# Where the operands of the spatial products lie in SBUF, and the order of work at the stage's two borders

## The chip, the cores and the metric

The kernel runs on one NeuronCore of a Trainium2 chip. The metric is the device time of one execution in microseconds (us). Of the kernel before there are three timed runs, with a median of 613.38 us (613.30 to 613.72), and one profiled execution.

## The reference

Two branches read the same normalised input and are added to it. All tensors are float32; there are S = 2048 rows, D = 512 columns, H = 32 heads of 16, and Fh = 688 gate columns.

```python
xn = layernorm(x)
# branch A: linear attention with a learned feature map
q, k, v = heads(xn @ wqkv)
phi(t) = concat(softmax(t @ w_phi), softmax(-(t @ w_phi)))     # per head
o = phi(q) @ (phi(k).T @ v) / (phi(q) @ sum_s(phi(k)) + 1e-6)
a = o @ wo
# branch B: spatial gate
z = gelu(xn @ w_in)                                            # 2 x 688 columns
z2 = layernorm(z[:, 688:])
g = w_sp @ z2 + b_sp[:, None]                                  # 2048 x 2048 by 2048 x 688
b = (z[:, :688] * g) @ w_out
out = x + a + b
```

The spatial product `w_sp @ z2` is the largest one.

## The kernel before, in words

**Arithmetic.** Every large product is made of three matmuls (`mm3`, lines 55 to 59): each operand is split into a rounded part h and a rest l, and hh, hl and lh are summed in PSUM. ScalarE rounds (`round_h`, line 49 of the profile), VectorE subtracts for the rest (`rest_l`, line 53). In a matmul the left operand is the 128x128 weight that is loaded into the array, and the right one is streamed through it.

**Stages.** The first stage makes the projections q, k and v of all 16 row tiles, the softmaxes, the sums over k, and the first gate half z1, which is kept in DRAM. The second (lines 737 to 768) makes z2, row tile by row tile: four PSUM pools in turn take the projection `zps` (`zproj`), ScalarE applies gelu, VectorE takes the statistics, GpSimd the reciprocal root, ScalarE normalises (`normed`). The third is the spatial stage (lines 887 to 926), with the products `g`. The last (lines 1075 to 1103) makes the two output projections into `pout`, and the attention's `po`.

**The spatial stage.** It uses Strassen's scheme in Winograd's form: 2x2 blocks of the left matrix with 2x2 blocks of the right one need seven products instead of eight. There are 32 chunks n. Eight groups i of 256 output rows have four quarters q each; chunk n is (i, q), and the last group takes its quarters in the order 1, 2, 3, 0 (`SEQ`, line 590). One chunk is seven products with two contraction steps k of three matmuls: 42 matmuls of 344 columns. `FORM` (line 776) gives the order: P1 = A11 B11, P2 = A12 B21, P6 = S2 T2, P5 = S1 T1, P7 = S3 T3, P3 = S4 B22, P4 = A22 T4. Seven of the eight PSUM banks hold the sums of a group, and the next group begins in the eighth.

**Left operands.** `load_a(n)` brings the chunk's two raw blocks over SP's DMA queue, and `prep_a(n)` makes from them A11, A12, A22 and the sums S1 to S4, in h and l. The raw blocks have two buffers. The finished tiles have two rooms, `hl[0]` (in the pool `ws`, at the right end of SBUF) for even n and `hl[1]` (at the end of the left pools) for odd n, so chunk n + 2 overwrites chunk n. The sums are made in a tile of their own, `S`.

**Right operands.** `b_split` makes B11, B21, B22 and T1 to T4 out of two finished row tiles of z2, for each of eight pairs of row tiles (2q + k). A B tile (`b_tile`, lines 694 to 703) is 5632 bytes of each partition: h and l, each with two operands of 344 columns of which every one has 352 words, that is 1408 bytes. Ten of the tiles are in the pools `xz2a` and `xz2`, five each; sixteen in the room of `xT` as it comes free; two in `xz3`.

**Order.** The program is traced in the order of the code; a scheduler then orders the instructions of each engine by its own cost model, gives out the slots of the pools, and sets the semaphores. A tile waits until all that used its room before is done. `tc.issue_after(ins)` puts the instructions of a block behind `ins` on the same engine.

**Drain.** When a group is done, ScalarE and VectorE combine its seven sums into four blocks (`drain`), `gate` multiplies them with gelu of z1, and the result goes through DRAM in transposed form for the last stage. During the last four chunks the last stage's first weights and operands are loaded (`stage_w`, `first_gate`), and the room of the left pools behind `xz` becomes the pools `cw` and `cwk`.

Of the kernel before, what the change touches and what calls it, by code (L numbers as in the profile page):

```python
# [10 lines left out]
F32 = mybir.dt.float32  # L11
# [7 lines left out]
P = 128  # L19
# [22 lines left out]
def mixer(ctx: ExitStack, tc: tile.TileContext, x, x_t, wv, wqkT, phi_bd, wo, w_in, wst, b_r, w_out, out):  # L42
# [50 lines left out]
    cst.tile([P, 8], F32, name="pad")  # L93
# [44 lines left out]
    def zproj(ps, s, w, order=(0, 1), wide=False):  # L138
# [405 lines left out]
    mid.enter_context(right("pad", 1)).tile([P, P + 8], F32, name="pad")  # L544
# [5 lines left out]
    w2_pool.tile([P, QP // 2], F32, name="gap")  # L550
# [45 lines left out]

    def load_a(n):
        i, q = SEQ[n]
        f = []
        for k in range(2):  # L600
            t = ws.tile([P, QC, P], F32, tag=f"f{k}", bufs=2, name="wf")
            sp.dma_start(t, wst[2 * i + k, :, q * QC:(q + 1) * QC, :])
            f.append(t.rearrange("p (k two) t -> p two k t", two=2))
        return f

    def prep_a(n, f):

# [10 lines left out]
        sums = (sm[0].tile([P, 4, 2, P], F32, name="S") if sm else  # L618
                zw.tile([P, 4, FC], F32, tag=("T", "z2")[n], bufs=n + 1, name="S").rearrange("p a b -> p (a b)")[:, :8 * P].rearrange("p (a k b) -> p a k b", a=4, k=2))
        parts(("A11", "A12"), a)  # L620
        dve.tensor_tensor(sums[:, 0], b[:, 0], b[:, 1], op=ALU.add)
        dve.tensor_tensor(sums[:, 1], sums[:, 0], a[:, 0], op=ALU.subtract)  # L622
# [7 lines left out]
    hl, raw, A, sm = [ws, None], {}, {}, []  # L630
    NE = 2
    with ExitStack() as p1:
# [40 lines left out]
        A[0] = prep_a(0, raw.pop(0))  # L673
        sp.dma_start(kvT_d, kvT)
# [30 lines left out]
    B, b11 = [], None  # L705

    def b_split(z, n):
        nonlocal b11
        tt = zw.tile([P, 4, FC], F32, tag="T", name="T")
        dve.tensor_tensor(tt[:, 0:2], z[:, 1:3], z[:, 0:2], op=ALU.subtract)  # L710
        if n % 2 == 0:
            b11 = b_tile()
        b_parts(b11[:, 0, n % 2], b11[:, 1, n % 2], z[:, 0])
        dve.tensor_tensor(tt[:, 2], z[:, 2], tt[:, 0], op=ALU.subtract)
# [23 lines left out]
    for s in range(NT):  # L738
        p = zproj((kv_ps_p, zc, zbp, za)[s % 4], s, w2, (0, 1) if s % 2 == 0 else (1, 0), s == 0)
# [397 lines left out]
```

## Time and profile before

| what | value |
| --- | --- |
| median of three runs | 613.38 us |
| the profiled execution, its own time | 613.14 us |
| its span, from first to last instruction | 611.4 us |
| TensorE busy | 605.8 us (99%) |
| TensorE weight loads busy | 551.9 us (90%) |
| VectorE busy | 519.9 us (85%) |
| ScalarE busy | 259.7 us (42%) |
| GpSimd busy | 132.4 us (22%) |
| granted TensorE clock | 1.00 throughout |

The busy time of an engine is the union of its instructions' times. A matmul of 344 columns is listed with some 319 ns and one of 512 with some 390 ns, but matmuls overlap in a pipeline: the next one starts long before the one before it has ended. What a matmul costs is the distance from its start to the next one's, which is called the beat here. It is read from the timeline, whose rows give start, duration, engine, line, operation, written and read tiles, shapes, a count, and the idle time of the engine before it with the instruction that ended it.

### The profile page before, as it was taken

What the parts mean: (1) busy time and instruction counts of PE and PEld (TensorE: products, weight loads), DVE (VectorE), ACT (ScalarE), POOL (GpSimd) and SP (SyncE); (2) the same over time, 40 slices, a digit from 0 to 9 for tenths busy, and PEclk for the clock granted to TensorE, in tenths of its full rate; (3) what the DMA queues carried; (4) which work ended last, traced back from release to release, by engine and by line L of the source; (5) the groups of instructions that cost most, each with busy time, mean ns of one, the idle gap of its engine ahead of it and who ended that gap; (6) DMA issues with size and microseconds to landing.
All of it is one profiled execution on the core that took longest, in us unless ns stands there. A gap on an engine that the chain in (4) does not pass through costs nothing.

```text
span 611.4 us, 11387 instructions
## 1 busy us (share of the span) xinstructions
PE 605.8 (99%) x4286; PEld 551.9 (90%) x4286; DVE 519.9 (85%) x930; ACT 259.7 (42%) x414; POOL 132.4 (22%) x231
## 2 busy tenths in 40 slices
PE   8999999999999999999999999999999999999997
PEld 7888888888888999999999999999999978777776
DVE  5999999999988578899888896877879999999932
ACT  4653324423433547887534434342345443332220
POOL 4122232323111014552000001000200041143430
PEclk9999999999999999999999999999999999999999
DMA  8557776566537848001445636455566799699882
GB/s 316 191 130 178 215 178 188 146 166 167 142 102 218 259 179 306 5 1 35 143 122 154 172 100 184 135 164 152 167 161 202 247 314 269 186 288 278 210 217 69
DMA packets 57950, 107.85 MB, mean 176 GB/s; under 512 B 12392, under 2 KB 24552, under 8 KB 57672
## 3 DMA queue, kind: packets, MB, share of 16 engines
q1 hardware_dynamic: 43656, 65.22, 34.6%
q0 software_dynamic: 11936, 36.28, 23.9%
q10 hardware_dynamic: 2304, 5.64, 2.4%
q8 instruction: 33, 0.54, 0.4%
q14 instruction: 21, 0.17, 0.1%
HBM read 66.85 MB, written 35.54 MB: 167 GB/s over the span
## 4 chain that ended last, share of the span: by engine, by line
PE 96%; DVE 1%; DMA 1%; issue 0%; POOL 0%; ACT 0%; POOLq 0%
PE g L57 12%; PE g L58 11%; PE g L59 11%; PE proj L57 7%; PE proj L58 7%; PE proj L59 7%; PE zps L57 6%; PE zps L59 6%; PE zps L58 6%; PE pout L57 6%; PE pout L59 5%; PE pout L58 5%; PE po L1003 1%; PE pout L1017 1%; DMA zacc<-e 1%; PE kvps L373 1%
## 5 line engine op out<-in xcount | busy, mean ns | idle before, releaser
L57 PE MATMUL g<-B,A 128*128 128x344 f32 x448 | 142.4, 319 | 0.0
L58 PE MATMUL g<-B,A 128*128 128x344 f32 x448 | 142.4, 319 | 0.0
L59 PE MATMUL g<-B,A 128*128 128x344 f32 x448 | 138.9, 318 | 0.0
L57 PEld LDWEIGHTS g<-B,A 128*128 128x128 f32 x448 | 84.1, 188 | 0.3 <-ACT A L49 0.3
L58 PEld LDWEIGHTS g<-B,A 128*128 128x128 f32 x448 | 84.0, 188 | 0.0
L59 PEld LDWEIGHTS g<-B,A 128*128 128x128 f32 x448 | 83.6, 188 | 0.0
L49 ACT ACTIVATE A<-S 128x512 fp32r<-128x512 f32 x64 | 39.3, 628 | 73.7 <-DVE S L622 54.1
L57 PE MATMUL proj<-wqk_h,xT 128*128 128x512 f32 x128 | 50.1, 391 | 0.0
L59 PE MATMUL proj<-wqk_h,xT 128*128 128x512 f32 x128 | 49.8, 389 | 0.0
L58 PE MATMUL proj<-wqk_l,xT 128*128 128x512 f32 x128 | 49.8, 389 | 0.0
L125 ACT ACTIVATE e<-e,r_x 128x1024 f32<-128x1024 f32 x26 | 29.8, 1149 | 42.3 <-DVE e L124 41.3
L53 DVE TENSOR_TENSOR A<-S,A 128x512 fp32r<-128x512 f32 x64 | 42.8, 683 | 2.9 <-ACT A L49 2.8
L49 ACT ACTIVATE A<-wf 128x512 fp32r<-128x512 f32 (+1 forms) x64 | 32.8, 515 | 25.4 <-DMA wf<-in_wst 20.8
L57 PE MATMUL zps<-w1h,xT 128*128 128x344 f32 (+2 forms) x128 | 40.8, 320 | 0.0
L59 PE MATMUL zps<-w1h,xT 128*128 128x344 f32 (+2 forms) x128 | 40.7, 318 | 0.0
L57 PE MATMUL zps<-w2h,xT 128*128 128x344 f32 (+2 forms) x128 | 40.7, 318 | 0.0
L58 PE MATMUL zps<-w1l,xT 128*128 128x344 f32 (+2 forms) x128 | 40.6, 318 | 0.0
L58 PE MATMUL zps<-w2l,xT 128*128 128x344 f32 (+2 forms) x128 | 40.6, 317 | 0.0
L59 PE MATMUL zps<-w2h,xT 128*128 128x344 f32 (+2 forms) x128 | 40.3, 317 | 0.0
L53 DVE TENSOR_TENSOR A<-wf,A 128x512 fp32r<-128x512 f32 (+1 forms) x64 | 35.0, 549 | 4.8 <-ACT A L49 4.8
L128 DVE TENSOR_REDUCE sm<-e 128x64 f32<-128x1024 f32 x26 | 31.1, 1199 | 2.5 <-ACT e L125 2.5
L787 POOL DMA_DIRECT2D z1t<-z_d x16 | 9.1, 595 | 108.6 <-DMA wf<-in_wst 98.1
(219 smaller groups left out, 1434.9 us busy)
## 6 DMA issues: line engine op xcount, KB each, us to landing
wf<-in_wst SPq DMA_DIRECT2D x64, 256.0 KB, 3.4
e_d<-e POOLq DMA_DIRECT2D x16, 544.0 KB, 5.0
et<-e_d SPq DMA_DIRECT2D x16, 544.0 KB, 7.6
z_d<-z1f ACTq DMA_DIRECT2D x16, 344.0 KB, 3.4
z1t<-z_d POOLq DMA_DIRECT2D x16, 344.0 KB, 4.6
zacc<-e POOLq DMA_DIRECT2D x10, 512.0 KB, 4.8
u<-u_d SPq DMA_DIRECT2D x15, 320.0 KB, 6.2
xt<-in_x SPq DMA_DIRECT2D x16, 256.0 KB, 3.7
```

What stands on the lines that cost most here:

```text
L49: return act.activation(h, src, AF.Copy).ins
L53: return (eng or dve).tensor_tensor(l, src, h.bitcast(F32), op=ALU.subtract).ins
L57: pe.matmul(dst, ah, bh, start=start, stop=False)
L58: pe.matmul(dst, ah, bl, start=False, stop=False)
L59: return pe.matmul(dst, al, bh, start=False, stop=stop).ins
L125: softmax_pair.last = less, act.activation(e, e, AF.Exp, scale=scale).ins
L128: dve.tensor_reduce(sm, heads(e), axis=AX.X, op=ALU.add)
L373: i = pe.matmul(kv_acc[k:k + QP, m // 4], vs[:, m * QP:(m + 1) * QP], e[:, m * HP:(m + 1) * HP], start=first and m < 4 and len(ready) == n ...
L787: pool.dma_start(t[:, k, :FH], z1_d[2 * i + k])
L1003: lasts[3] = pe.matmul(po[r][c * QP:(c + 1) * QP, k], kvT[rows, m // 2, cols], fs[m // 4][rows, m // 2 % 2], start=True, stop=True).ins
L1017: lasts[2] = pe.matmul(p, rt, w, start=False, stop=i == NT - 1 and k == 1).ins
```

## The change

It has four parts.

1. **Addresses.** Some paddings get other sizes: the constants' pad of 8 words goes, the pad at the right end of SBUF shrinks from 136 to 16 words, the gap at the end of `w2` grows from 16 to 48 words, and a pad of 32 words stands ahead of `hl[1]`. Within a chunk the left operands are laid out in another order, S4 S3, A22, A11 A12, S2 S1, with 32 words more in the tile of A11 and A12, where A11 starts 32 words later when the quarter is even. `spread` changes one step of an access pattern. Of the right operands, B21 now comes first in its tile and B22 second, and a tile of B11 is shared by the quarters q and q + 1 of the same k, and not by the two k of one quarter.
2. **Sums in place.** S1 to S4 are written over the raw blocks, once A11, A12 and A22 have been rounded. The tile `S` goes. There are three raw tiles (f and x in `ws`, y in the room of `zw`) and loads are asked for four chunks ahead, not three.
3. **The border between second and third stage.** The left operands of chunks 1 and 2 are prepared ahead of the last three normalisations and the last two splits, and chunk 0's products are traced ahead of these. The third raw load is traced earlier, behind chunk 0's preparation. The first subtraction of a late split is put behind chunk 1's sums.
4. **Drain and last stage.** The block c22 is made of P7 and c12, no longer of P5 and c21. The PSUM pool of the last stage's output is opened first, with its first tile, and the pool of transposes behind it. The tiles of the pool `cw` come in another order.

```diff
-    cst.tile([P, 8], F32, name="pad")
...
-    mid.enter_context(right("pad", 1)).tile([P, P + 8], F32, name="pad")
+    mid.enter_context(right("pad", 1)).tile([P, HP // 4], F32, name="pad")
...
-    w2_pool.tile([P, QP // 2], F32, name="gap")
+    w2_pool.tile([P, QP + HP // 4], F32, name="gap")
...
+    def spread(ap, axis, more):
+        dims = [list(d) for d in ap.ap]
+        dims[axis][0] += more
+        return bass.AP(ap.tensor, ap.offset, dims)
+
     def load_a(n):
         i, q = SEQ[n]
-        f = []
+        tag = "fx"[n] if n < 2 else "fxy"[(n - 2) % 3]
+        t = (fy[0] if tag == "y" else ws).tile([P, 2, QC, P], F32, tag="wf" + tag, name="wf")
         for k in range(2):
-            t = ws.tile([P, QC, P], F32, tag=f"f{k}", bufs=2, name="wf")
-            sp.dma_start(t, wst[2 * i + k, :, q * QC:(q + 1) * QC, :])
-            f.append(t.rearrange("p (k two) t -> p two k t", two=2))
-        return f
+            sp.dma_start(t[:, k], wst[2 * i + k, :, q * QC:(q + 1) * QC, :])
+        return [t[:, k].rearrange("p (k two) t -> p two k t", two=2) for k in range(2)]
...
+        for names, more in ((("S4", "S3"), 0), (("A22",), 0), (("A11", "A12"), QP), (("S2", "S1"), 0)):
+            tiles[names] = pl.tile([P, D * len(names) + more], F32R, tag="".join(names), name="A")
+
         def parts(names, src):
-            t = pl.tile([P, 2, len(names), 2, P], F32R, tag="".join(names), name="A")
-            prep_a.last = b_parts(t[:, 0], t[:, 1], src)
+            late = QP * (1 - SEQ[n][1] % 2) if "A11" in names else 0
+            more = QP if "A11" in names else 0
+            t = tiles[names][:, late:late + D * len(names)].rearrange("p (m l k t) -> p l m k t", l=2, k=2, t=P)
+            h, l = (spread(t[:, v], 1, more - late) for v in range(2))
+            prep_a.last = b_parts(h, l, src)
             for k, m in enumerate(names):
-                ops[m] = t[:, 0, k], t[:, 1, k]
+                ops[m] = h[:, k], l[:, k]
...
         parts(("A11", "A12"), a)
-        dve.tensor_tensor(sums[:, 0], b[:, 0], b[:, 1], op=ALU.add)
-        dve.tensor_tensor(sums[:, 1], sums[:, 0], a[:, 0], op=ALU.subtract)
-        parts(("S1", "S2"), sums[:, 0:2])
-        dve.tensor_tensor(sums[:, 2], a[:, 0], b[:, 0], op=ALU.subtract)
-        dve.tensor_tensor(sums[:, 3], a[:, 1], sums[:, 1], op=ALU.subtract)
-        parts(("S3", "S4"), sums[:, 2:4])
         parts(("A22",), b[:, 1:2])
+        a11, a12, a21, a22 = a[:, 0], a[:, 1], b[:, 0], b[:, 1]
+        dve.tensor_tensor(a22, a21, a22, op=ALU.add)
+        dve.tensor_tensor(a21, a11, a21, op=ALU.subtract)
+        dve.tensor_tensor(a11, a22, a11, op=ALU.subtract)
+        prep_a.summed = dve.tensor_tensor(a12, a12, a11, op=ALU.subtract).ins
+        parts(("S2", "S1"), pair(a11, a22))
+        parts(("S4", "S3"), pair(a12, a21))
...
         A[0] = prep_a(0, raw.pop(0))
+        prep_a.first = None
+        raw[2] = load_a(2)
         sp.dma_start(kvT_d, kvT)
...
-        if n % 2 == 0:
-            b11 = b_tile()
-        b_parts(b11[:, 0, n % 2], b11[:, 1, n % 2], z[:, 0])
+        k, q = n % 2, n // 2 % 2
+        if not q:
+            b11[k] = b_tile()
+        b = b11[k][:, 0, q], b11[k][:, 1, q]
+        b_parts(*b, z[:, 0])
...
-        if s == NT - 1:
-            for k in range(2):
-                normed(*late.pop(0), ins)
     ctx_w2.__exit__(None, None, None)
     x3.append(mid.enter_context(ctx_x3))
     hl[1] = mid.enter_context(left("hl1", 1))
+    hl[1].tile([P, QP], F32, name="pad")
     A[1] = prep_a(1, raw.pop(1))
-    raw[2] = load_a(2)
-    normed(*late.pop(), ins)
-    ctx_zw.__exit__(None, None, None)
+    prep_a.first = prep_a.summed
+    raw[3] = load_a(3)
...
+    products(0, g)
+    A[2] = prep_a(2, raw.pop(2))
+    while late:
+        normed(*late.pop(0), ins)
+    ctx_zw.__exit__(None, None, None)
+    gt = mid.enter_context(right("gt", 1))
+    fy.append(mid.enter_context(right("fy", 1)))
...
         dve.tensor_tensor(c12, g["P5"], c21, op=ALU.add)
+        add(c22, g["P7"], b2, c12)
         dve.tensor_tensor(c21, g["P7"], c21, op=ALU.add)
-        add(c22, g["P5"], b2, c21)
...
-    er_pair("er")
-    wo_h = cw.tile([P, ND, D], F32R, name="woh")
+    f_pair()
+    cw.tile([P, KF * P], F32, tag="u", bufs=4, name="u")
     cw.tile([2 * REM, P], F32R, tag="rt", bufs=6, name="rt")
+    wo_l = cw.tile([P, ND, D], F32R, name="wol")
     cw.tile([P, D], F32, tag="wof", bufs=4, name="wof")
     kvT = cw.tile([P, 2 * NG, HP], F32, name="kvT")
-    cw.tile([P, KF * P], F32, tag="u", bufs=4, name="u")
-    wo_l = cw.tile([P, ND, D], F32R, name="wol")
+    wo_h = cw.tile([P, ND, D], F32R, name="woh")
...
+    pso = ctx.enter_context(psum("pso", 1))
+    pout = [pso.tile([P, D], F32, tag="out", bufs=2, name="pout")]
     pst = ctx.enter_context(psum("pst", 4))
-    pso = ctx.enter_context(psum("pso", 1))
```

More of the change, by code (lines that the diff above doesn't have):

```diff
@@ L136, in mixer, with zproj @@
     za = ctx_z.__enter__()
-    def zproj(ps, s, w, order=(0, 1), wide=False):
+    def zproj(ps, s, w, wide=False):
         if ps in (za, kv_ps_p):
@@ L153, in zproj @@
             return list(zip(parts, dst))
-        for k, j in enumerate(order):
+        for k in range(2):
             for c in range(ND):
                 cs = slice(c * P, (c + 1) * P)
-                zproj.last = mm3(p[k][:, :FC], (t[:, 0, cs], t[:, 1, cs]), (w[j][0][:, c], w[j][1][:, c]), c == 0, c == ND - 1)
+                zproj.last = mm3(p[k][:, :FC], (t[:, 0, cs], t[:, 1, cs]), (w[k][0][:, c], w[k][1][:, c]), c == 0, c == ND - 1)
         if ps in (za, kv_ps_p):
@@ L610, in prep_a, with pair @@
         ops = {}
+        tiles = {}
+        for names, more in ((("S4", "S3"), 0), (("A22",), 0), (("A11", "A12"), QP), (("S2", "S1"), 0)):
+            tiles[names] = pl.tile([P, D * len(names) + more], F32R, tag="".join(names), name="A")
         def parts(names, src):
[L613 to L614 removed]
+            late = QP * (1 - SEQ[n][1] % 2) if "A11" in names else 0
[3 more added lines that the diff above has]
+            prep_a.last = b_parts(h, l, src)
             for k, m in enumerate(names):
[L616 to L619 removed]
+                ops[m] = h[:, k], l[:, k]
+        def pair(x, y):
+            (first, kd, td), more = x.ap, y.offset - x.offset
+            return bass.AP(x.tensor, x.offset, [first, [more, 2], kd, td])
         parts(("A11", "A12"), a)
[L621 to L627 removed]
+        parts(("A22",), b[:, 1:2])
+        a11, a12, a21, a22 = a[:, 0], a[:, 1], b[:, 0], b[:, 1]
[5 more added lines that the diff above has]
+        parts(("S4", "S3"), pair(a12, a21))
         return ops
[L630 removed]
+    hl, raw, A, fy = [ws, None], {}, {}, []
     NE = 2
@@ L703, in b_tile @@
         return t.rearrange("p (a b c) -> p a b c", a=2, b=2)[..., :FC]
-    B, b11 = [], None
+    B, b11 = [], [None] * 2
     def b_split(z, n):
-        nonlocal b11
         tt = zw.tile([P, 4, FC], F32, tag="T", name="T")
-        dve.tensor_tensor(tt[:, 0:2], z[:, 1:3], z[:, 0:2], op=ALU.subtract)
-        if n % 2 == 0:
-            b11 = b_tile()
-        b_parts(b11[:, 0, n % 2], b11[:, 1, n % 2], z[:, 0])
-        dve.tensor_tensor(tt[:, 2], z[:, 2], tt[:, 0], op=ALU.subtract)
-        ops = {"B11": (b11[:, 0, n % 2], b11[:, 1, n % 2])}
+        with tc.issue_after(prep_a.first) if prep_a.first else ExitStack():
+            dve.tensor_tensor(tt[:, 0:2], z[:, 1:4:2], z[:, 0:2], op=ALU.subtract)
+        k, q = n % 2, n // 2 % 2
[3 more added lines that the diff above has]
+        b_parts(*b, z[:, 0])
+        dve.tensor_tensor(tt[:, 2], z[:, 3], tt[:, 0], op=ALU.subtract)
+        ops = {"B11": b}
         t = b_tile()
         b_parts(t[:, 0], t[:, 1], z[:, 2:4])
-        ops["B22"], ops["B21"] = [(t[:, 0, k], t[:, 1, k]) for k in range(2)]
-        dve.tensor_tensor(tt[:, 3], z[:, 3], tt[:, 2], op=ALU.subtract)
+        ops["B21"], ops["B22"] = [(t[:, 0, k], t[:, 1, k]) for k in range(2)]
+        dve.tensor_tensor(tt[:, 3], z[:, 2], tt[:, 2], op=ALU.subtract)
         t = b_tile()
@@ L738, in mixer @@
     for s in range(NT):
-        p = zproj((kv_ps_p, zc, zbp, za)[s % 4], s, w2, (0, 1) if s % 2 == 0 else (1, 0), s == 0)
+        p = zproj((kv_ps_p, zc, zbp, za)[s % 4], s, w2, wide=s == 0)
         if s < NT - 2:
@@ L890, in mixer @@
             z = load_z1(i)
-        products(n, g)
+        if n:
+            products(n, g)
         if n % NQ == NQ - 1 and i < NP - 1:
@@ L896, in mixer @@
             g = {}
-        if n + 3 < NC:
-            raw[n + 3] = load_a(n + 3)
-        if n + 2 < NC:
+        if n + 4 < NC:
+            raw[n + 4] = load_a(n + 4)
+        if 0 < n < NC - 2:
             A[n + 2] = prep_a(n + 2, raw.pop(n + 2))
@@ L1012, in project_u @@
         uh, ul, rt = u
-        p = pso.tile([P, D], F32, tag="out", bufs=2, name="pout")
+        p = pout.pop() if pout else pso.tile([P, D], F32, tag="out", bufs=2, name="pout")
         for c in range(KF):
```

15 lines of the change are left out of this document (7 added, 8 removed).

## The prediction

> **What bounds the kernel now.** First the page: engines, TensorE clock, and the chain that ended last.
>
> ```profile
> PE   8999999999999999999999999999999999999997
> PEclk9999999999999999999999999999999999999999
> PE 96%; DVE 1%; DMA 1%; issue 0%; POOL 0%; ACT 0%; POOLq 0%
> PE g L57 12%; PE g L58 11%; PE g L59 11%; PE proj L57 7%; PE proj L58 7%; PE proj L59 7%; PE zps L57 6%; PE zps L59 6%; PE zps L58 6%; PE pout L57 6%; PE pout L59 5%; PE pout L58 5%; PE po L1003 1%; PE pout L1017 1%; DMA zacc<-e 1%; PE kvps L373 1%
> ```
>
> TensorE is the chain (96%) at its full clock, and the spatial products `g` are 34% of it. Only two things count: the beat of its matmuls (start to start; the page's 319 ns is one matmul's latency in a pipeline) and its pauses. I read the beat from the timeline, whose first column is the start in us. The spatial stage runs from the first row below to the last:
>
> ```profile
> 275.66 0.32 PE L57 MATMUL g<-B,A 128*128 128x344 f32 x1
> 486.01 0.32 PE L59 MATMUL g<-B,A 128*128 128x344 f32 x1
> 486.44 0.47 PE L57 MATMUL pout<-wu,u_uh 128*128 128x512 f32 x1
> ```
>
> That is 486.44 - 275.66 = 210.78 us for 3 x 448 = 1344 matmuls. The projection before it has the same width, 344:
>
> ```profile
> 262.01 0.32 PE L58 MATMUL zps<-w2l,xT 128*128 128x344 f32 x1
> 275.51 0.32 PE L59 MATMUL zps<-w2h,xT 128*128 128x344 f32 x1
> ```
>
> 88 steps in 13.50 us: 153.4 ns (starts repeat 0.46 us per three, so 153.33). In `g` it depends on the place. One odd chunk (n = 19) and one even (n = 20):
>
> ```profile
> 402.64 0.32 PE L57 MATMUL g<-B,A 128*128 128x344 f32 x1
> 404.33 0.32 PE L59 MATMUL g<-B,A 128*128 128x344 f32 x1
> 404.49 0.32 PE L57 MATMUL g<-B,A 128*128 128x344 f32 x1
> 405.28 0.32 PE L59 MATMUL g<-B,A 128*128 128x344 f32 x1
> 409.17 0.32 PE L57 MATMUL g<-B,A 128*128 128x344 f32 x1
> 410.91 0.32 PE L59 MATMUL g<-B,A 128*128 128x344 f32 x1
> ```
>
> From 402.64, P6 and P5, 12 matmuls: 1.69/11 = 153.6 ns. From 404.49, P7: 0.79/5 = 158. From 409.17, again P6 and P5: 1.74/11 = 158.2. So two things slow the beat. P7's operands disagree: a B tile's second half starts 352 x 4 = 1408 bytes on, 128 off modulo 256, while all left operands lie at multiples of 512 bytes from their tile's start, which has the B tiles' phase. Second halves hold B21, T3, T4 and every other B11, so 7 of 14 pairs disagree. P6 and P5 agree in both chunks, and in the even one still run slow after disagreeing P2: the beat has a memory. The projections show it without any disagreement:
>
> ```profile
> 204.22 0.50 PE L650 MATMUL pz<-zhl,ones_r 128*128 128x512 f32 x1 [0.22 <-DVE zhl L53]
> 204.56 0.32 PE L57 MATMUL zps<-w1h,xT 128*128 128x344 f32 x1
> 211.98 0.32 PE L59 MATMUL zps<-w1h,xT 128*128 128x344 f32 x1
> 212.52 0.32 PE L58 MATMUL zps<-w1l,xT 128*128 128x344 f32 x1
> 215.99 0.32 PE L59 MATMUL zps<-w1h,xT 128*128 128x344 f32 x1
> ```
>
> After a wait at 204.22, 47 steps of 7.42/47 = 157.9 ns, and after transposes 22 of 157.7; it came back only after the 512-wide matmuls behind. So agreeing operands keep the beat that they have: 153.33 when they follow running matmuls, 157.8 after a break.
>
> **The change, part by part.** *Agreement.* The constants lose 32 bytes, so B and `xT` move 32 down. Odd chunks' A tiles start 128 higher against B (`hl1`'s pad). Even ones: the right edge's pad shrinks by 480 bytes, the A tiles take 128 more, so they start 352 higher, which is 128 + 224, and 224 up is 32 down modulo 256. Hence S3, S4 and A22 stand 128 off B's base, where T3, B22 and T4 now are; S1, S2 and A12, behind another 128, meet first halves; A11 takes the 128 only for even quarters, as B11 does. All 14 pairs agree, and `w2` (-480 + 128 + 128 = -224) keeps its phase to `xT`. The stage starts right behind `zps` at 153.33. If nothing breaks it: 1344 x 153.33 = 206.08 us, 4.70 less than 210.78. That includes three pauses, the third being 486.44 - 486.01 - 0.15 = 0.28:
>
> ```profile
> 294.33 0.32 PE L59 MATMUL g<-B,A 128*128 128x344 f32 x1
> 294.62 0.43 PE L57 MATMUL g<-B,A 128*128 128x344 f32 x1
> 294.89 0.32 PE L58 MATMUL g<-B,A 128*128 128x344 f32 x1
> 463.57 0.38 PE L57 MATMUL g<-B,A 128*128 128x344 f32 x1
> 463.79 0.32 PE L58 MATMUL g<-B,A 128*128 128x344 f32 x1
> ```
>
> (0.29 - 0.15) + (0.27 - 0.15) = 0.26 and 0.22 - 0.15 = 0.07. So the pauses are 0.61 and the beat is 4.09.
>
> [...]
>
> *Sums in place, strided sources.* Four adds and four rounded pairs per chunk remain. In-place and strided operands cost nothing in these rows (mean ns behind the comma):
>
> ```profile
> L622 DVE TENSOR_TENSOR S<-S,wf 128x256 f32<-128x256 f32 x32 | 13.3, 416 | 0.0
> L621 DVE TENSOR_TENSOR S<-wf 128x256 f32<-128x256 f32 x32 | 13.3, 415 | 9.5 <-DMA wf<-in_wst 7.4 <-PE kvt L662 2.0
> L53 DVE TENSOR_TENSOR A<-S,A 128x512 fp32r<-128x512 f32 x64 | 42.8, 683 | 2.9 <-ACT A L49 2.8
> L53 DVE TENSOR_TENSOR A<-wf,A 128x512 fp32r<-128x512 f32 x32 | 21.9, 684 | 3.5 <-ACT A L49 3.5
> ```
>
> The raw tile stays held until the last pair, so a load starts some 2 us later, but there are three raw tiles for two and loads are asked one chunk earlier. On SP's queue the third load now stands ahead of the stores of `kvT` and `zb`; it waits for chunk 0's last copy, and behind it wait the two feature loads, which VectorE needs: at worst some 2 us in a stage where TensorE has no use for them. I take 0; cover is VectorE's slack below.
>
> *Drain.* The last reader of P5 was the sixth VectorE operation, and now is the fourth; P7's goes from fifth to sixth. The 0.22 step at 463.57 is where the next round needs P5's bank. P7's bank is needed 6 x 153 ns = 0.92 us later than that, so it should be ready: -0.07.
>
> *Border.* VectorE's load decides. In the table by stretches the pairs behind the length are TensorE, its weight loads, VectorE:
>
> ```profile
> 275.70:295.00 19.30, 19.30 (x123) 19.04 (x122) 17.66 (x37) 12.98 (x22) 4.76 (x8) 1.00 0.21 66
> 350.00:376.00 26.00, 26.00 (x168) 26.00 (x168) 21.14 (x45) 9.38 (x17) 1.49 (x3) 1.00 0.46 129
> ```
>
> It is busy 92% of the time in the first stretch, 81% later. What an operation takes from the next one is its distance in starts:
>
> ```profile
> 283.56 0.86 DVE L53 TENSOR_TENSOR B<-T,B 128x688 fp32r<-128x688 f32 x1
> 284.35 0.86 DVE L53 TENSOR_TENSOR B<-z,B 128x688 fp32r<-128x688 f32 x1
> 288.13 0.50 DVE L714 TENSOR_TENSOR T<-z,T 128x344 f32<-128x344 f32 x1
> 288.56 0.86 DVE L53 TENSOR_TENSOR B<-T,B 128x688 fp32r<-128x688 f32 x1
> 298.55 0.68 DVE L53 TENSOR_TENSOR A<-wf,A 128x512 fp32r<-128x512 f32 x1
> 299.15 0.68 DVE L53 TENSOR_TENSOR A<-S,A 128x512 fp32r<-128x512 f32 x1
> ```
>
> So 0.79 at 688 columns, 0.43 at 344, 0.60 at 512, and 0.416 - 0.08 = 0.34 at 256. A chunk is 3 x 0.60 + 5 x 0.34 = 3.5 us, a B split 4 x 0.79 + 3 x 0.43 = 4.45. Chunks 1 to 3 and the last two splits make 19.4 us. Chunk 3's sums are needed at 275.66 + 3 x 6.44 + 1.84 = 296.8, some 20 us after VectorE turns to this work (about 277). It fits by a hair. Deferring the three normalisations puts what chunks 1 and 2 need first, and chunk 3's splits last. Bounds: -0.26 (the pause goes) to +1.5 (VectorE at 92% of 20 us does 18.6, short by 0.8, and a late load of the third raw tile as much again). I take -0.26.
>
> *Last stage.* Output banks now come first: the first takes the eighth bank, which no product of the last round holds, so -0.28. The room's new order adds no instruction. Its bounds are 0 and the rival below; I take 0.
>
> Sum: -4.09 - 0.26 - 0.07 - 0.28 = -4.70; the span 611.4 becomes 606.7, the profiled execution 613.14 becomes 608.4, and the median, 0.24 above it, 613.38 becomes **608.7 us**.
>
> **The rivals.** *Slow beat (the other side).* One pause near the border breaks the good beat, and nothing in the stage, all 344 wide, restores it. Broken after k matmuls the stage takes 153.33k + 157.8(1344 - k); that passes 210.78 at k = 291, or 320 us. Broken at the second chunk (k = 42): 42 x 0.1533 + 1302 x 0.1578 + 0.26 = 212.15, +1.4 with the last pause already left out: **614.8**; at 294: 614.4. For: 69 steps at 157.8 without recovery. Against: the early loads and deferred splits.
>
> *VectorE paces the border* but the beat survives: 1.5 us given back, 610.2. For: 92%. Against: the margin after 350.
>
> *Late room.* B tiles of the last quarter are now shared so that eight, not seven, live to the end; then only two of five tiles of the second pool are free for the three stagings of `w_out`, and the third waits for the last chunk's P7, 1.84 us before its end.
>
> ```profile
> wof<-in_w_out SPq DMA_DIRECT2D x5, 256.0 KB, 4.1
> 479.85 0.37 SPq L971 DMA_DIRECT2D kvT<-kvT_d x1
> 490.52 1.09 PE L1003 MATMUL po<-f,kvT 64*32 64x256 f32 x32
> ```
>
> A load of 4.1 and copies of 1.3 end 3.6 us behind the stage; if `kvT`'s room lies behind it, its load (4 more) lands at 7.6, against a need at 490.52 - 486.44 = 4.1: +3.5, 612.2. Against: other tiles can be picked.
>
> *Nothing but pauses:* the disagreement is not the cause, or the addresses don't come out as worked above: -0.61, 612.8. Against: P6 and P5 in odd chunks.
>
> **How the numbers follow.** Forecast 0.50 (own range 608.0 to 609.4: a stray break, 0.7, above; an unpriced saving below), slow beat 0.15, VectorE 0.13, late room 0.14, only pauses 0.08. Below 613.4 lie all but the slow beat and some of the late room. About 0.2% (1.2 us) is what a measurement of this kernel can tell from no change. Faster by more: 0.50 + 0.13 + half of late room, 0.70. Slower by more: most of the slow beat with later pauses, 0.12. Within: 0.18.
>
> **What would show it.** Right: P7, P2 and P4 at 0.46 us per three matmuls, the whole stage in 206 us, no idle or long step at 294, 463 and its end. Wrong: 0.47 to 0.48 per three from some point on (slow beat), with a step over 0.2 us just ahead; steps over 0.2 us without that (VectorE); a wait of `po` or `pout` on a load behind the stage (late room); a mix as before (only pauses).

## The result, and the profile after

The changed kernel takes **620.16 us** (median of six runs), the kernel before 613.34 us beside it. The ratio is 1.010, with a 95% interval of 1.0081 to 1.0118: slower by 1.0%, where the prediction said 0.8% faster. The forecast 608.7 is missed by 11.5 us, and the time lies outside the range. One of the six executions (752.86 us, mean clock 0.754) ran at three quarters of the clock from its first microseconds on, and it was the profiled one; it is left out, and the trace shown here as the profile after is that of a further execution of the same kernel (the first run below: 622.25 us, span 620.2).

First the page of the changed kernel, engines, clock and chain, as they were shown of before.

```profile
PE   8999999999999999999899999999999979999997
PEclk9999999999999999999989999999999989999999
PE 77%; DVE 6%; DMA 5%; issue 4%; POOL 3%; ACT 3%; SPq 2%; ACTq 0%; POOLq 0%; DVEq 0%
```

Before, the chain was TensorE at 96% and the clock was full in every slice. Now TensorE is 77% of the chain, and two slices have an 8 in the clock line, the first just behind the slice in which TensorE falls to 8 tenths, the second in the one in which it falls to 7. The waits of TensorE (waiting line, releaser: us in total, times, longest) name the two places:

```profile
PE pout L57 <- ACT oT L49: 4.1, 1, 4.1
PE g L57 <- ACT A L49: 2.3, 1, 2.3
```

The table by stretches shows what follows each wait. After the length come the busy times of TensorE, its weight loads, VectorE, ScalarE and GpSimd, then the granted clock, the DMA share and GB/s.

```profile
275.81:301.40 25.59, 25.59 (x169) 25.59 (x168) 23.86 (x47) 16.12 (x28) 5.37 (x11) 1.00 0.27 89
...
304.77:308.19 3.42, 1.35 (x9) 1.07 (x7) 3.42 (x10) 0.44 (x1) 0.00 (x0) 1.00 0.00 0
308.19:315.01 6.82, 6.52 (x21) 6.08 (x22) 6.10 (x11) 3.21 (x5) 0.00 (x0) 0.50 0.22 68
...
376.00:488.90 112.90, 112.90 (x734) 112.90 (x733) 99.05 (x198) 46.93 (x81) 9.29 (x17) 1.00 0.58 169
495.92:499.33 3.41, 2.19 (x10) 1.48 (x8) 0.69 (x1) 0.63 (x1) 2.34 (x5) 1.00 0.92 242
499.33:502.75 3.42, 0.56 (x2) 0.49 (x3) 1.07 (x2) 1.60 (x3) 0.00 (x0) 1.00 0.90 253
502.75:506.16 3.41, 3.41 (x9) 2.67 (x8) 2.54 (x4) 0.74 (x1) 0.00 (x0) 0.50 0.96 352
```

The same stretch of the stage in the kernel before:

```profile
376.00:486.44 110.44, 110.33 (x707) 110.00 (x705) 93.80 (x195) 45.31 (x82) 8.37 (x16) 1.00 0.61 178
```

The reader is to see two things. From 376 to the stage's end TensorE runs without a pause at 112.90/733 = 154.0 ns, where the row of before (110.44 us, 706 steps) gives 156.4: the agreement works. And behind each wait there is a stretch at a granted clock of 0.50.

The timeline of TensorE shows the steps themselves:

```profile
305.80 0.31 PE L58 MATMUL g<-B,A 128*128 128x344 f32 x1
308.43 0.66 PE L57 MATMUL g<-B,A 128*128 128x344 f32 x1 [2.32 <-ACT A L49]
308.89 0.49 PE L58 MATMUL g<-B,A 128*128 128x344 f32 x1
309.18 0.49 PE L57 MATMUL g<-B,A 128*128 128x344 f32 x1
309.46 0.49 PE L58 MATMUL g<-B,A 128*128 128x344 f32 x1
...
488.81 0.32 PE L59 MATMUL g<-B,A 128*128 128x344 f32 x1
488.96 0.39 PE L57 MATMUL pout<-wu,u_uh 128*128 128x512 f32 x1
...
497.48 0.63 PE L1038 MATMUL pout<-wu,u 96*128 96x512 f32 x2
502.19 0.50 PE L57 MATMUL pout<-woh,oT 128*128 128x512 f32 x1 [4.08 <-ACT oT L49]
502.53 0.43 PE L58 MATMUL pout<-wol,oT 128*128 128x512 f32 x1
502.76 0.63 PE L57 MATMUL pout<-woh,oT 128*128 128x512 f32 x1
503.18 0.63 PE L58 MATMUL pout<-wol,oT 128*128 128x512 f32 x1
503.61 0.63 PE L59 MATMUL pout<-woh,oT 128*128 128x512 f32 x1
```

In the half-clock stretches the 344-wide starts at 308.89, 309.18 and 309.46 are 0.29 and 0.28 us apart, and the 512-wide ones at 502.76, 503.18 and 503.61 0.42 and 0.43. Against the forecast's span of 606.73 (275.66 ahead of the stage, 206.08 in it, 124.99 behind it) this execution's 620.17 divides as follows, each number from starts in the two traces, the last row as what remains:

| part | forecast | trace after | difference |
| --- | --- | --- | --- |
| ahead of the first `g` | 275.66 | 275.81 | +0.15 |
| beat of `g`: mean of 1321 undisturbed steps 154.25 ns, not 153.33 | 206.08 | 207.29 | +1.2 |
| pauses at 305.8 to 310.5 (2.48 and three small ones) | 0 | 3.07 | +3.1 |
| 21 steps at half clock, 0.13 us longer each | 0 | 2.80 | +2.8 |
| pause at 497.7 (4.48 to the next start, less one step of 0.23) | 0 | 4.25 | +4.25 |
| nine steps behind it at half clock | 0 | 1.70 | +1.7 |
| rest of the last stage | 124.99 | 125.26 | +0.3 |

Together 13.4. The change also gives up the alternating order of the two halves in the second stage's projection (`order` in `zproj`), which the list of its four parts leaves out; the first row says that the stages ahead take the same time without it.

The executions differ in their mean granted clock: this one has 0.991, the five of the first comparison have 0.993 to 0.996, and the median lies 2 us lower. What lies around the span has grown too, from 1.7 (613.14 - 611.4) to 2.05 us (622.25 - 620.2). It is about 2.05 in every run below that has the whole change and about 1.75 in the two that start from the kernel before, so some 0.3 us belong to the change; the cause is not shown.

### The profile page after: what moved, and what is told of

The parts are those of the page before. It is cut to its first block, busy times and chain, and to the rows that moved or that the text cites. A ratio compares the mean times of both kernels' runs of the same rounds, so it can differ in the third digit from the quotient of the medians.

```text
span 750.8 us, 11374 instructions
## 1 busy us (share of the span) xinstructions
PE 742.7 (99%) x4286; PEld 633.6 (84%) x4286; DVE 532.9 (71%) x930; ACT 264.9 (35%) x414; POOL 130.2 (17%) x231
## 4 chain that ended last, share of the span: by engine, by line
PE 97%; SPq 1%; DMA 0%; issue 0%; ACT 0%; DVE 0%; POOL 0%; ACTq 0%; POOLq 0%
PE g L57 11%; PE g L59 11%; PE g L58 11%; PE proj L59 7%; PE proj L58 7%; PE proj L57 7%; PE zps L57 7%; PE zps L59 7%; PE zps L58 7%; PE pout L57 5%; PE pout L59 5%; PE pout L58 5%; PE kvps L372 1%; PE po L1024 1%; SPq L869 1%; PE pout L1038 1%
## 5 line engine op out<-in xcount | busy, mean ns | idle before, releaser
L58 PE MATMUL g<-B,A 128*128 128x344 f32 x448 | 161.6, 363 | 0.0
L57 PE MATMUL g<-B,A 128*128 128x344 f32 x448 | 161.2, 363 | 0.0
L59 PE MATMUL g<-B,A 128*128 128x344 f32 x448 | 156.5, 362 | 0.0
L49 ACT ACTIVATE A<-wf 128x512 fp32r<-128x512 f32 (+1 forms) x128 | 71.0, 574 | 139.1 <-PE g L59 84.9
L53 DVE TENSOR_TENSOR A<-wf,A 128x512 fp32r<-128x512 f32 (+1 forms) x128 | 77.7, 620 | 44.3 <-ACT A L49 44.0
L58 PEld LDWEIGHTS g<-B,A 128*128 128x128 f32 x448 | 88.7, 198 | 1.7
L57 PEld LDWEIGHTS g<-B,A 128*128 128x128 f32 x448 | 88.4, 198 | 1.7
L59 PEld LDWEIGHTS g<-B,A 128*128 128x128 f32 x448 | 88.3, 198 | 1.6
L59 PE MATMUL proj<-wqk_h,xT 128*128 128x512 f32 x128 | 60.1, 470 | 0.0
L57 PE MATMUL proj<-wqk_h,xT 128*128 128x512 f32 x128 | 57.8, 451 | 0.0
L116 DVE TENSOR_REDUCE mm<-proj 128x32 f32<-128x512 f32 x32 | 22.0, 688 | 38.5 <-PE proj L59 38.5
L57 PE MATMUL zps<-w1h,xT 128*128 128x344 f32 (+2 forms) x128 | 46.9, 368 | 0.0
L57 PE MATMUL zps<-w2h,xT 128*128 128x344 f32 (+2 forms) x128 | 46.7, 365 | 0.0
L59 PE MATMUL zps<-w1h,xT 128*128 128x344 f32 (+2 forms) x128 | 46.6, 364 | 0.0
L59 PE MATMUL zps<-w2h,xT 128*128 128x344 f32 (+2 forms) x128 | 46.1, 363 | 0.0
L57 PE MATMUL pout<-wu,uh 128*128 128x512 f32 x75 | 35.4, 472 | 0.0
L59 PE MATMUL pout<-wu,ul 128*128 128x512 f32 x75 | 34.8, 463 | 0.0
```

Source lines behind the costliest of these rows:

```text
L49: return act.activation(h, src, AF.Copy).ins
L53: return (eng or dve).tensor_tensor(l, src, h.bitcast(F32), op=ALU.subtract).ins
L57: pe.matmul(dst, ah, bh, start=start, stop=False)
L58: pe.matmul(dst, ah, bl, start=False, stop=False)
L59: return pe.matmul(dst, al, bh, start=False, stop=stop).ins
L116: dve.tensor_reduce(mm[:, 0], heads(src), axis=AX.X, op=ALU.max)
```

## The experiments

The kernels beside which each was timed are the kernel before on the same chip (median 614.1 for the first four, 614.3 for the next three, 614.2 and 613.8 for the last two pairs). The three runs from the raw tiles' turn to the half-agreeing kernel with both edits were taken on another chip than the rest, so across that border the ratios are compared, not the medians.

### The changed kernel again

No edit.

> The changed kernel unchanged, for a trace at its usual pace. Two theories share the 11.4 us between the forecast 608.7 and the measured 620.2. Clock theory: operands that agree everywhere make TensorE's work denser, and the granted clock falls below 1.000 (mean 0.994, worth some 3.7 us); the g beat is 153.33 ns wherever the clock is full, and 344-wide matmuls outside the spatial stage run at the lower clock too. Room theory: the four loads of wo begin only behind the last product, and TensorE stands still 2 to 6 us at the start of the last stage. Rival, slow beat: one pause breaks the beat, the g matmuls run at 157.8 ns over most of the stage (212 us) with the clock at 1.000.

Measured: 620.69 us, ratio 1.0113 (1.0085 to 1.014). The rows are above. The room theory holds: TensorE stands 4.1 us on `oT`. The clock theory falls in the form it was told: at 376 to 488.9, where the agreeing operands run most densely, the clock is 1.00, and while TensorE still has work it is 0.50 only behind the two pauses. The slow beat falls too: outside the disturbed steps the mean is 154.25 ns, not 157.8.

That gave a new theory, called pause and window in what follows: a pause is paid twice, once as itself, and once more as a stretch at half clock when TensorE has been idle for most of a stretch of 3.41 us (2.07 and 2.86 us in the two rows ahead of the falls). The stretches lie on a grid in this trace: the two falls of the clock stand at 308.19 and 502.75, and the 194.56 us between them are 57 times 3.413.

### Half of the pairs disagree again

The left operands return to the phase of before; all other edits stay.

```
-    mid.enter_context(right("pad", 1)).tile([P, HP // 4], F32, name="pad")
+    mid.enter_context(right("pad", 1)).tile([P, HP // 4 + QP], F32, name="pad")
...
-    w2_pool.tile([P, QP + HP // 4], F32, name="gap")
+    w2_pool.tile([P, HP // 4], F32, name="gap")
...
-        for names, more in ((("S4", "S3"), 0), (("A22",), 0), (("A11", "A12"), QP), (("S2", "S1"), 0)):
+        for names, more in ((("S4", "S3"), 0), (("A22",), 0), (("A11", "A12"), 0), (("S2", "S1"), QP)):
...
-            late = QP * (1 - SEQ[n][1] % 2) if "A11" in names else 0
-            more = QP if "A11" in names else 0
+            late, more = 0, QP if "A11" in names else 0
...
-            h, l = (spread(t[:, v], 1, more - late) for v in range(2))
+            h, l = (t[:, v] for v in range(2))
...
-    hl[1].tile([P, QP], F32, name="pad")
```

> The changed kernel with the left operands back at the phase of before: half of the product pairs (7 of 14) 128 bytes off modulo 256, everything else as changed. Clock theory: the granted clock returns to 1.000, the g beat to 156.4 ns, so -3.7 and +4.1: about 620 to 621. If the clock does not depend on where operands lie: clock still 0.994, and 624. If places don't matter at all: 620 with the g beat as in the changed kernel.

Measured: 622.94 us, ratio 1.0154 (1.0126 to 1.0181), 2.3 us more than the kernel above. Clock 0.994, with stretches of 0.50 behind the same two pauses, although half of the pairs disagree: the half clock does not hang on all of them agreeing.

### All pairs disagree

Only the three pads, so that the left operands as a whole stand 128 bytes further; the rest of the edit above is left out.

```
-    mid.enter_context(right("pad", 1)).tile([P, HP // 4], F32, name="pad")
+    mid.enter_context(right("pad", 1)).tile([P, HP // 4 + QP], F32, name="pad")
...
-    w2_pool.tile([P, QP + HP // 4], F32, name="gap")
+    w2_pool.tile([P, HP // 4], F32, name="gap")
...
-    hl[1].tile([P, QP], F32, name="pad")
```

> The changed kernel with all 14 pairs 128 bytes off modulo 256 (the left operands moved by 128 bytes as a whole). If disagreement sets the slow beat: all g matmuls at 157 to 158 ns, stage about 212 us. Clock theory: clock 1.000 and 622; if the clock does not depend on the places: 0.994 and 626; if places don't matter at all: 620.

Measured: 624.82 us, ratio 1.0184 (1.0153 to 1.0214). Expected was some 626, since the clock is still 0.994. The same instructions from 376 to the end of the stage, with half and with no pair agreeing:

```profile
376.00:491.60 115.60, 115.60 (x741) 115.60 (x740) 100.45 (x200) 47.69 (x83) 9.29 (x17) 1.00 0.58 167
...
376.00:492.20 116.20, 116.20 (x741) 116.20 (x740) 99.97 (x200) 47.78 (x83) 9.29 (x17) 1.00 0.58 166
```

115.60/740 = 156.2 ns and 116.20/740 = 157.0, against 154.0 with all pairs agreeing. Half clock stands behind both pauses here too (from 311.21 and from 505.77), so it does not need agreeing operands at all. But the place sets the beat, and the three kernels stand in the order 620.7, 622.9, 624.8. Only distances of 0 and 128 bytes were tried; that the period is 256 was the author's estimate, not shown by a run of its own; the three kernels fit it. Between all pairs and none the rows differ by 3 ns of 157 a matmul. By what path the place acts is not shown.

### The last stage's room in another order

```
     f_pair()
     cw.tile([P, KF * P], F32, tag="u", bufs=4, name="u")
+    kvT = cw.tile([P, 2 * NG, HP], F32, name="kvT")
+    cw.tile([P, D], F32, tag="wof", bufs=4, name="wof")
     cw.tile([2 * REM, P], F32R, tag="rt", bufs=6, name="rt")
     wo_l = cw.tile([P, ND, D], F32R, name="wol")
-    cw.tile([P, D], F32, tag="wof", bufs=4, name="wof")
-    kvT = cw.tile([P, 2 * NG, HP], F32, name="kvT")
     wo_h = cw.tile([P, ND, D], F32R, name="woh")
```

> The changed kernel with one reordering of the last stage's room: kvT and the four staging tiles of wo now lie on room that is free long before the last product, rt and wol on the room of the last B tiles. Room theory: the loads of wo begin some 480 to 490 us into the run as in the kernel before, no wait of TensorE behind the last product over 1 us, 2 to 6 us less: 614 to 618. If the wait is hidden or something else is late at the same place: no change, 620. The clock stays what it is in the changed kernel.

Measured: 616.08 us, ratio 1.0032 (1.0019 to 1.0046): 4.6 us less than the changed kernel, as the room theory said. In the changed kernel SP's queue and ScalarE show why `oT` was late:

```profile
488.54 0.33 SPq L991 DMA_DIRECT2D kvT<-kvT_d  x1
488.92 9.09 SPq L869 DMA_DIRECT2D wof<-in_wo  x16
...
501.02 0.63 ACT L49 ACTIVATE woh<-wof 128x512 fp32r<-128x512 f32 x1 [2.76 <-DMA wof<-in_wo]
501.56 1.07 ACT L49 ACTIVATE oT<-po 128x512 fp32r<-128x512 f32 x2
```

`kvT` and most of the four staging tiles of `wo` lie on B tiles that the last products read, so the sixteen loads begin at 488.9, take 9 us to issue, the last copy of `wo` waits for the last of them, and `oT` stands behind that copy on ScalarE. With the new order the same queue reads

```profile
482.55 0.37 SPq L991 DMA_DIRECT2D kvT<-kvT_d  x1
482.98 9.32 SPq L869 DMA_DIRECT2D wof<-in_wo  x16
```

and the wait of 4.1 us is gone (0.6 us remain, on a feature tile). The pause near 306 stays, with its half clock:

```profile
305.79:309.20 3.41, 1.01 (x5) 0.61 (x4) 3.41 (x9) 1.44 (x3) 0.00 (x0) 1.00 0.00 0
309.20:312.62 3.42, 3.27 (x11) 3.27 (x12) 3.29 (x7) 2.21 (x3) 0.00 (x0) 0.50 0.04 11
```

### The raw tiles in another turn

```
-        tag = "fx"[n] if n < 2 else "fxy"[(n - 2) % 3]
+        tag = "fxfx"[n] if n < 4 else "fyx"[(n - 4) % 3]
```

> The changed kernel with the raw tiles taken in another turn: chunk 4 takes the first tile again (free once chunk 2 is made), chunk 5 the new third tile, whose room is VectorE's last normalised tile. New theory (pause and window): the fourth load stood at the head of SP's queue until the last B split, TensorE paused 2.0 to 2.6 us at 306, and a stretch of 3.41 us with more than some 2 us of idle TensorE is followed by 3.41 us (once 6.83 us) at half clock. Then both go with this edit: no pause over 1 us near 306, no half clock behind it, the stage some 208 us instead of 213, about 5 us less than the changed kernel: 615 to 616; the pause of 4 us behind the last product and its half clock stay. Clock theory as told first (the power of agreeing operands): half clock stays at 308, and 3 us at most are won. If VectorE's load is the cause and not the load's turn: pause stays, 620.

Measured: 618.67 us, ratio 1.0061 (1.0037 to 1.0086). By the two ratios (1.0113 and 1.0061) that is 3.2 us less than the changed kernel, where about 5 had been expected. The stage went from 213.15 to 207.94 us as expected, with no half clock in it; the pause behind the last product stayed, and in this trace 6.82 us at half clock followed it (496.64 to 503.46), not 3.41.

The mechanism that the expectation told was wrong in one detail. The order of the loads on SP's queue, as read from the built programs, is

```
changed kernel:   chunk 3, chunk 5, chunk 4, chunk 6
with this edit:   chunk 3, chunk 4, chunk 5, chunk 6
```

The scheduler had put chunk 5's load ahead of chunk 4's, because chunk 5 takes the tile that chunk 2 frees and chunk 4 the third tile, in the room of the last normalised z2. The traces do not name a load's chunk, but the semaphores in them fit: the A22 that is rounded first is tied to the last of the four loads of chunks 4 and 5 (two of 256 KB each) in the changed kernel, and to the second with this edit. The times of issue hardly differ: the four go out within 1.8 us, from 294.5 in the changed kernel and from 295.3 here. What differs is which of them is awaited first. ScalarE, whose 256-wide operations are the A22 of a chunk, waits for them; first the changed kernel, then this one:

```profile
303.08 1.26 ACT L49 ACTIVATE A<-wf 128x256 fp32r<-128x256 f32 x3 [2.64 <-DMA wf<-in_wst]
307.75 0.63 ACT L49 ACTIVATE A<-wf 128x512 fp32r<-128x512 f32 x1 [3.42 <-DVE wf L637]
```

```profile
299.55 0.41 ACT L49 ACTIVATE A<-wf 128x256 fp32r<-128x256 f32 x1
300.91 0.63 ACT L49 ACTIVATE A<-wf 128x512 fp32r<-128x512 f32 x1 [0.95 <-DMA wf<-in_wst]
302.77 0.42 ACT L49 ACTIVATE A<-wf 128x256 fp32r<-128x256 f32 x1 [1.22 <-DMA wf<-in_wst]
305.53 1.15 ACT L49 ACTIVATE A<-wf 128x512 fp32r<-128x512 f32 x2 [2.34 <-DVE wf L637]
```

Chunk 4's A22 is ready at 300 instead of 303, its first pair of sums is rounded at 305.5 instead of 307.8, and the pause at 306 shrinks from 2.48 to 0.47 us.

### Both edits

> Both edits: the raw tiles' turn and the room of kvT and wo's staging tiles. Pause and window theory: no pause over 1 us behind 275 us, granted clock 1.000 up to the last instruction, stage about 207 us, 611 to 612 and so faster than the kernel before (613.4) by 1.5 to 2.5 us. Power theory: a half clock somewhere though there is no pause, 613 or more.

(The power theory is the clock theory of the first run.)

Measured: **611.57 us**, ratio 0.9959 (0.9938 to 0.9979): faster than the kernel before, at a granted clock of 1.000. Run once more on another occasion (below) it gave 611.65, ratio 0.9969. The single executions spread from 609.8 to 615.9 us, all at a clock of 1.000; no trace shows why. In this trace TensorE still paused at the border, for 1.3 us where none over 1 us was expected, and the rows show what the pause did to the beat:

```profile
305.69 0.31 PE L59 MATMUL g<-B,A 128*128 128x344 f32 x1
307.18 0.43 PE L57 MATMUL g<-B,A 128*128 128x344 f32 x1 [1.17 <-ACT A L49]
...
308.38 0.32 PE L58 MATMUL g<-B,A 128*128 128x344 f32 x1
308.76 0.42 PE L57 MATMUL g<-B,A 128*128 128x344 f32 x1
...
309.17 0.32 PE L57 MATMUL g<-B,A 128*128 128x344 f32 x1
309.32 0.32 PE L58 MATMUL g<-B,A 128*128 128x344 f32 x1
309.48 0.32 PE L59 MATMUL g<-B,A 128*128 128x344 f32 x1
```

From 309.17 on the steps are 0.15 and 0.16 again, after two breaks, and six steps from 407.48 to 408.40 take 0.92 us, 153.3 ns each: all-344 work found its good beat back. The pause of 1.3 us (a step of 1.49 less one of 0.15) left the clock at 1.00.

### Both edits, half of the pairs disagreeing

The edits of the two runs above and those of the second run.

> Both edits, and the left operands back at the phase of before (7 of 14 pairs disagree). Prices agreement by itself where nothing pauses: the mean beat back from 154.25 to 156.4 ns, 1344 x 2.15 = 2.9 us more than the kernel with both edits: 614 to 615. If agreement is worth nothing outside the pauses: the same 611 to 612.

Measured: 614.02 us, ratio 1.0006 (0.9988 to 1.0025). Against both edits alone (0.9959) the agreement is worth 0.0047 of the time, 2.9 us, as expected; with the two intervals it lies between some 1 and 4.6 us. Without it the rest of the change is worth nothing that can be measured. The agreement alone, in the kernel before, was not run.

### The late room alone, in the kernel before

```
     er_pair("er")
-    wo_h = cw.tile([P, ND, D], F32R, name="woh")
+    cw.tile([P, KF * P], F32, tag="u", bufs=4, name="u")
     cw.tile([2 * REM, P], F32R, tag="rt", bufs=6, name="rt")
+    wo_l = cw.tile([P, ND, D], F32R, name="wol")
     cw.tile([P, D], F32, tag="wof", bufs=4, name="wof")
     kvT = cw.tile([P, 2 * NG, HP], F32, name="kvT")
-    cw.tile([P, KF * P], F32, tag="u", bufs=4, name="u")
-    wo_l = cw.tile([P, ND, D], F32R, name="wol")
+    wo_h = cw.tile([P, ND, D], F32R, name="woh")
```

> The kernel before with one line group of the change alone: its last stage's room in the changed order, so that kvT and most staging tiles of wo lie on a B tile that is read up to the last product (486). Half of its pairs disagree, and nothing paused in it so far. Room theory with pause and window: the wo loads begin at 486 instead of 480, TensorE pauses about 4 us some 9 us behind the last product, 3.41 us at half clock follow (1.7 us more), together +5 to +7: 618.5 to 620.5. If half clock needs the agreeing operands: the pause alone, +4, clock 1.000. If the border of the changed kernel is what makes wo late: no change, 613.4.

### Three of four staging tiles late, in the kernel before

```
     er_pair("er")
     wo_h = cw.tile([P, ND, D], F32R, name="woh")
+    cw.tile([P, KF * P], F32, tag="u", bufs=4, name="u")
+    kvT = cw.tile([P, 2 * NG, HP], F32, name="kvT")
     cw.tile([2 * REM, P], F32R, tag="rt", bufs=6, name="rt")
     cw.tile([P, D], F32, tag="wof", bufs=4, name="wof")
-    kvT = cw.tile([P, 2 * NG, HP], F32, name="kvT")
-    cw.tile([P, KF * P], F32, tag="u", bufs=4, name="u")
     wo_l = cw.tile([P, ND, D], F32R, name="wol")
```

> The kernel before with the last stage's room in an order that puts three of the four staging tiles of wo on late room, and leaves kvT and the first staging tile on early room: 12 of the 16 loads wait for the last product, so the last copy of wo is some 2.3 us earlier than with all of them. A smaller dose of the same pause: about 1.5 to 2 us, and by the stretches seen so far (up to 1.90 us of idle TensorE in a stretch of 3.41 us left the clock alone, 2.23 us halved the next one) no half clock if it is under 2 us: 615 to 616. If any pause over 1 us halved the clock: 617 to 618.

Measured: 620.03 us, ratio 1.008 (1.0053 to 1.0107), and 618.66 us, ratio 1.0082 (1.005 to 1.0115). The first is as the room theory said: this one line group costs the kernel before 4.9 us by the ratio (0.008 of 614.2), half-clock stretches included. In its trace the clock is 1.00, so the pause alone (3.1 us) is what that execution shows. The second missed as a smaller dose: TensorE waited 3.0 us, against 3.1 in the first, since the last copy of `wo` was no earlier (497.50 and 497.72). But the two traces show nearly the same pause with a different clock behind it; first the late room, then three of four late. In the second the clock falls at 498.88, which gives the stretches' borders; in the first it does not fall, and the borders in its rows are the author's estimate. In the traces in which the clock falls the nearest stretches are 1.7 us idle (clock kept) and 2.0 us (clock halved), not the 1.90 and 2.23 of the expectation.

```profile
494.00:497.41 3.41, 1.75 (x8) 1.12 (x6) 0.69 (x1) 0.55 (x1) 0.25 (x1) 1.00 0.73 196
497.41:500.83 3.42, 1.95 (x8) 1.61 (x9) 3.15 (x5) 2.15 (x5) 0.00 (x0) 1.00 0.96 337
500.83:504.24 3.41, 3.41 (x17) 2.82 (x16) 3.21 (x7) 1.61 (x3) 0.27 (x1) 1.00 1.01 370
```

```profile
495.46:498.88 3.42, 0.47 (x3) 0.21 (x2) 0.72 (x2) 1.38 (x3) 0.00 (x0) 1.00 0.93 320
498.88:502.29 3.41, 3.41 (x9) 2.62 (x9) 3.16 (x4) 1.01 (x3) 0.00 (x0) 0.50 1.03 368
```

Within one stretch (2.95 us idle) the pause halved the next; in the first trace the clock stayed at 1.00, and if the borders are right, the pause was split over two stretches there (1.66 and 1.47 us idle). The first kernel's other four executions had a mean clock of 0.994 to 0.997, against 0.999 to 1.000 in ten of the eleven of the kernel before beside it, so there it probably did fall; they have no trace. Half of these kernels' pairs disagree, and nothing else of the change is in them.

### A further order on VectorE

Chunk 5's A22 is rounded behind chunk 4's last pair (`issue_after` on both engines), on top of both edits; beside it both edits once more.

```
-        rest_l(l, src, h)
+        b_parts.rest = rest_l(l, src, h)
...
-        parts(("A22",), b[:, 1:2])
+        with ExitStack() as st:
+            if n == 5:
+                st.enter_context(tc.issue_after(prep_a.rest))
+                st.enter_context(tc.issue_after(prep_a.last))
+            parts(("A22",), b[:, 1:2])
...
         parts(("S4", "S3"), pair(a12, a21))
+        prep_a.rest = b_parts.rest
```

> Both edits, and chunk 5's lone left operand (A22) rounded only behind chunk 4's last pair, on ScalarE and on VectorE. In the trace with both edits TensorE still paused 1.3 us at 305.7, because VectorE stood 2.0 us at 302.2 with chunk 5's A22, whose load had not landed, ahead of chunk 4's sums. Theory: the order on VectorE's queue is what is left of the border's pause; it goes below 0.5 us, the stage takes about 207.3 us instead of 208.8, 610 to 611. Rival: the loads themselves are late (six of 256 KB within 13 us), then the pause only moves to chunk 5's or 6's products and the time stays at 611.5.

> The kernel with both edits once more, beside the one with the further order, on the same chip: 611 to 612, faster than the kernel before by 1.5 to 2.5 us, and up to 1.3 us slower than the one with the further order.

Measured: 612.76 us, ratio 0.9974 (0.9958 to 0.9991), and 611.65 us, ratio 0.9969 (0.9949 to 0.9989). The time missed the 610 to 611 expected, and the two kernels do not differ. The pause at 305.7 is gone with the further order, but one of 0.4 us stands at 312.3 instead, in chunk 5's products, as the rival had it. Beside it the kernel with both edits paused only 0.4 us at 305.5 in this trace, where it had paused 1.3 us in the one before, so the length of that pause varies between executions. The stage took 207.7 us with the further order and 208.2 without it, but in the last stage, at 512, TensorE waited 1.0 us on `oT` with it and 0.2 without. Late loads stay possible, and what is left of the border is not settled. Both kernels are faster than the one before by 0.1 to 0.5%.

## Why the prediction was wrong

**Agreement: right, but mis-sized.** The term was -4.09 at a beat of 153.33 ns. Measured: 154.25 against 156.40 in the traces (-2.89 over 1344 matmuls), -2.9 us between the kernels with both edits. So the rival "nothing but pauses" falls. The full gain needs every step at 153.33; chunks that TensorE takes one after the other come near it (153.4 for chunk 20 in the kernel with both edits), those where it takes the matmuls of two products in turn do not (155.1 and 155.8 for the 42 matmuls, counted by start, of chunks 18 and 19). Those alternate between operands whose phases differ by 128 although each pair agrees; that this is the reason is argued, not shown.

**"Agreeing operands keep the beat that they have": wrong.** It rested on two stretches of projections, of 47 and 22 steps. In the stage the beat came back after each break, so the slow-beat rival, which needed 1302 slow matmuls, did not come about.

**Drain and output bank: right.** No step over 175 ns is left at the round's end that stood at 463.57, and `pout` follows the last `g` by 0.15 us (488.81 to 488.96). Together a third of a microsecond.

**"Sums in place, strided sources ... I take 0": wrong in two ways.** The durations are the same, but four sums in place depend on each other. Where they stand back to back in the kernel before (made in a tile of their own) and in the one with the further order they start at

```profile
292.41 0.42 DVE L621 TENSOR_TENSOR S<-wf 128x256 f32<-128x256 f32 x1
292.75 0.42 DVE L624 TENSOR_TENSOR S<-wf 128x256 f32<-128x256 f32 x1
```

```profile
307.63 0.42 DVE L639 TENSOR_TENSOR wf<-wf 128x256 f32<-128x256 f32 x1
308.09 0.42 DVE L640 TENSOR_TENSOR wf<-wf 128x256 f32<-128x256 f32 x1
```

0.34 apart, and 0.46. In the kernel before the one pair in which the second sum reads what the first has just written (L622, L625) is 0.45 apart as well, and where the sums of two chunks alternate in the kernel with both edits, written in place too, they are 0.33 apart. So the extra time goes with the dependence and not with the place. The prediction read the means of the groups, which do not show it, and none of its rows has an operation that writes over its own source. No trace shows that these some 0.3 us of VectorE a chunk delayed TensorE. The larger error is the sentence on the loads: "the raw tile stays held ... but there are three raw tiles for two". The third tile's room belongs to the last z2, so at the border it is no third tile. The load of chunk 4 went behind that of chunk 5, and both behind chunk 2's last pair.

**Border: "I take -0.26"; measured +3.1 and +2.8 of half clock.** The bounds were -0.26 to +1.5. The rival "VectorE paces the border" named the place and a late load of the third raw tile as half of its price, but put the rest on VectorE's load; the run with the raw tiles' turn alone, with VectorE's work as it was, took 2.0 of the 2.5 us away. What is left is not settled.

**"The room's new order adds no instruction ... I take 0": the step that cost most,** 4.25 us of pause and 1.7 of half clock. The late-room rival (+3.5) had the mechanism, room of last-read B tiles under something that the last stage loads, but the wrong tile: the staging of `w_out` was in time. `kvT`, which it also named, was loaded 8.7 us later than in the kernel before (488.54 against 479.85), and `po` at 492.92 did not wait for it; the pause came from `wo`. The prediction had the order of the pool's tiles in the diff and the last readers of the B tiles in the trace; laying one over the other would have told it.

**No term for the clock.** The profile before has no pause over 0.3 us in the whole of these stages, so its clock line of nines said nothing of what a pause costs. Half clock took 2.8 + 1.7 us of the 13.4. And the rivals were given as alternatives; two of them came together.

## What to carry to other kernels

When a pool's tiles are reordered, lay their addresses over the last readers of what lay there, and follow the first load that waits through its queue to the engine behind it; a new order without a new instruction is not free. As these runs go, price a pause of a dense TensorE stage at its length plus up to half of each 3.41 us stretch that follows at half clock (2.80 us of 6.82 and 1.70 of 3.41 in the changed kernel), and expect nothing of the second part when the idle time within one such stretch stays well under 2 us (1.7 us left the clock at 1.00, 2.0 us halved it). Bringing the streamed and the loaded operand of the seven pairs that by the prediction's reckoning stood 128 bytes apart modulo 256 to the same place was worth 2.9 us of 211 here, and made the kernel faster only once the two pauses that the rest of the change brought were taken away.

## What the runs showed of the hardware

In the stretches listed from the experiments' traces the granted clock is 1.00 or 0.50. The stretches at half clock are 3.41 or 6.82 us long, and the two falls of a trace are 194.56 us apart in three runs, 57 times 3.413: at 308.19 and 502.75 in the changed kernel, at 311.37 and 505.93 with half of the pairs, at 311.21 and 505.77 with none. In the six traces in which the clock falls while TensorE still has work, a stretch of 3.41 us at full clock with up to 1.7 us of idle TensorE left the next one alone, and one with 2.0 us or more halved it. The two nearest rows are these, from the run with half of the pairs (the clock of the next stretch 1.00) and from that with none (0.50):

```profile
499.10:502.52 3.42, 1.70 (x8) 1.07 (x6) 0.17 (x1) 0.63 (x1) 1.25 (x3) 1.00 0.84 215
```

```profile
307.79:311.21 3.42, 1.40 (x7) 1.11 (x8) 3.42 (x9) 1.78 (x3) 0.00 (x0) 1.00 0.00 0
```

A half-clock stretch in which TensorE was idle for 0.3 us was followed by a second one (308.19 to 315.01 above); with 0.15 us idle (309.20, in the run with the room's new order) it stayed one stretch.

All-344 work, which the projections of before had shown at 157.7 to 157.9 ns after a break without recovery, came back in the spatial stage: in the run with both edits, behind the breaks at 305.69 and 308.38, to the 153.3 ns at 407.48 that are given there. The projections' own places are not what made them slow: in the trace of before fourteen other stretches of the same projection (`zps` from `w1`, between 40.60 and 202.99, 3 to 35 matmuls each) run at 153.3. What makes the difference is open.
